# One fused scan-and-attention kernel: wider VectorE operations, B transposed in SBUF, A's x in four transposes, PSUM banks by table, a new static order

## The chip, the cores and the metric

The kernel runs on one core of a Trainium2 chip. A core has five engines with a queue each: TensorE (PE; its weight loads are listed as PEld), VectorE (DVE), ScalarE (ACT), GpSimd (POOL) and SyncE (SP), which here issues almost all DMAs. They share the on-chip memory SBUF (128 partitions), and PE writes to PSUM, which has 8 banks of 512 f32 a partition. Each engine works through its own instructions in program order, and waits at an instruction until what it needs is there. The metric is the device time of one execution in microseconds (us), lower is better.

## The reference

Two independent blocks read their own x of 2048 x 448 in bf16; their outputs stand side by side in a 2048 x 896 result.

```python
# A: a diagonal complex state space, 448 states
B_bar = ((Lam_bar - 1.0) / Lam)[:, None] * Bmat        # Lam_bar = exp(exp(log_dt) * Lam)
Bu = jnp.einsum("bld,pd->blp", x + 0j, B_bar)
for t in range(L):                                     # L = 2048
    h = Lam_bar[None, :] * h + Bu[:, t, :]
y = 2.0 * jnp.einsum("blp,dp->bld", hseq, Cmat).real + x * Dskip
# B: dilated local attention, 16 heads of 28, 8 keys at distance 0, 2, .. 14
q, k, v = ...                                          # x @ wqkv
logits = jnp.einsum("bhsd,bhswd->bhsw", q, kg) * scale # kg: the 8 keys of each position
attn = softmax(where(mask, logits, -1e9))
o = jnp.einsum("bhsw,bhswd->bhsd", attn, vg)
out = o @ wo
```

The factor `(Lam_bar - 1) / Lam` belongs to a state, so it may stand on a row of B or on a column of C.

## The kernel before

Position s = 16 q + j: q is one of 128 rows, j one of 16 columns (T = 16). A group g is four columns, a batch b two groups; batch 1 (j 8 to 15) is done ahead of batch 0. Channels come in KT = 4 tiles, three of 128 and one of 64.

**Block B.** x is transposed by DMA column by column group (`load`, L361). PE projects Q and K (L478, L485, L511); ACT or DVE evicts them from PSUM (helpers `copy` and `evict`: L215 and L217 on ACT, L219 and L221 on DVE) into the tile qk. For each of the eight distances w, DVE multiplies Q by shifted K (`prod`, L651 to L657) into a ring of three buffers of 4096 elements; two distances make one unit. Where the shift leaves the first column, a unit falls into pieces, as the positions wrap to the row above. PE sums over the channels with a 0/1 matrix (`summ`, L669, L675: logits). Softmax of a batch: a maximum (DVE, L698), subtraction (PE), exp (ACT, L708, with a table load ahead of it), a sum (PE, into sm_ps), reciprocal and product (DVE, L717 and L719), and a transpose of the result by DMA (L724). V is projected (L757) and evicted to vd; `halo` copies the rows that wrap. In `pv` DVE multiplies attn by vd (L814) and adds the products up (L817, L826, L829), and PE multiplies the sum by wo (L888, L895).

**Block A.** The states come in NM = 7 groups m of 64, real above imaginary part. `setup` computes the powers on POOL and ACT: exp and Sin on ACT (L1078, L1081), the products on POOL; Gd is the block matrix of the factor. `setup_weights` (L1149) multiplies B by Gd on PE, 28 matmuls into ps_b (L1161), and 7 evictions make Bcat. `powers` (L1170) builds for each m the block matrices of 15 powers of Lam_bar in one DVE operation of 1920 elements (pw, L1177). `scan` (L1186) runs in levels: B times x for the four residues i of j modulo 4 (L1227, L1236), then combining steps on PE with pw (L1246, L1253, L1263, ... L1281), each followed by an eviction on ACT (L1243, L1250, L1260, L1267, L1274); then back down (L1298, L1317, L1323), where a bank that was given up is filled again by a matmul with the identity (L1303, L1317). Of the scan's small buffers (e1, eA, eB, ubuf) there are NF = 3 sets. C is transposed by DMA (L1004) straight into Ccat, and `outputs` (L1405) multiplies h by C (L1424), adds x times Dskip by a diagonal matrix Dg (built on ACT, L1132; L1420), and for j from 12 on by DVE (L1401, L1436).

**What sets the order.** Every piece of work is a unit in a planner (`add`, L116). The order of all engines is a written-out list ORDER: an entry's value modulo 1000 is the unit, and the thousands choose the engine where a unit may run on either. A unit that comes earlier in the list stands earlier on its engine. PSUM is one double bank (tag W: logits, the scan's pairs) and six single banks (tag s) in rotation.

```python
for i in ORDER:
    u = self.units[i % 1000]
    u.on = u.eng[i // 1000]
```

SP's queue holds, in this order: x of B with A's two B loads among it, A's x in 15 transposes of four blocks and one of a rest (L974, L969, L977), the small loads, wo, vd's halo, attn's transpose, C, and later the outputs.

Of the kernel before, what the change touches and what calls it, by code (L numbers as in the profile page):

```python
# [32 lines left out]
QW = 2 + NCH  # L33
LV2 = ((1, 2, 3), (4, 8, 12), (16, 32, 48))
# [4 lines left out]
NF = 3  # L39
# [166 lines left out]
class Ctx:  # L206
# [84 lines left out]
    def warm(self):  # L291

        nc, P = self.nc, self.plan
        self.pr = self.pool.tile([NCH, 3 * 4096], bf16, name="prods")
        self.pr_ring = Ring(3)
        self.pr_ring.get()
# [21 lines left out]
class PartB:  # L318
# [94 lines left out]
    def prep(self, u_warm):  # L413
# [135 lines left out]
        for b in (1, 0):  # L549
# [29 lines left out]
            self.k3[:, JB:T, 1:2], self.k3[:, JB:T, NCH:NCH + 1]), [self.u_k3[2], self.u_k3[3], self.u_kh[0], self.u_kh[1]], 0)  # L579

    def qk(self, b, prio):
        nc, pool, V, P, cx = self.nc, self.pool, self.nc.vector, self.plan, self.cx
        box = {}
# [5 lines left out]
        first = True  # L589
        for g in (2 * b + 1, 2 * b):  # L590
            par = g - 2 * b
            j0 = 4 * g
            for tp in (3, 2, 1, 0):
                ub = {}
                deps = list(self.u_q[b, par])
                ws = (W - 1 - 2 * tp, W - 2 - 2 * tp)
                for w in ws:
                    for j in range(j0, j0 + 4):
                        src = j - DIL * w
                        if src >= 0:  # L600
                            deps += self.u_k[src // 4]
                        else:
                            deps += self.u_k[(src + T) // 4] + [self.u_pad[(src + T) // 8]]
                w3 = () if tp > 1 else (ws[0] - 4, ws[1] - 4)
# [956 lines left out]
```

## Time and profile before

| what | value |
|---|---|
| median of 3 runs | 139.11 us (138.9 to 139.13) |
| span of the profiled execution | 136.8 us |
| granted TensorE clock | 1.00 |
| DMA, mean | 121 GB/s, 54.8% of 16 engines' span in its main queue |
| HBM read and written | 4.32 MB and 3.67 MB |

The profile is of one execution; its span is from the first to the last instruction and is 2.3 us less than the median of the runs. Of an engine the page gives busy time, its share of the span and the number of instructions; a row of 40 digits gives the busy share in tenths for each fortieth of the span (3.4 us). A group's row ends with busy time and the mean duration of one; where an engine overlaps its instructions, the step from one start to the next is shorter than that duration, and it is the step that counts in a sum.

### The profile page before, as it was taken

Reading aid. Unit: us, or ns where it says so; the run is one execution under the profiler, and the core shown is the slowest. Engines: PE = TensorE matmul, PEld = TensorE weight load, DVE = VectorE, ACT = ScalarE, POOL = GpSimd, SP = SyncE. Lnnn points to the kernel's source line nnn. Section 1 sums busy time; section 2 is a strip of 40 time slices with the busy share of each in tenths; the row PEclk is TensorE's granted clock in tenths of the full one; section 3 lists DMA queues with packets and bytes.
Section 4 is the critical chain, followed back from the end, with each engine's and each line's share of the span. In section 5 each row is a group of like instructions: output and inputs, shape, how many; then the busy total and the mean of one; then the engine's idle time right before and its main releaser. Section 6 shows DMA issues by size and latency. Waiting matters only on the chain.

```text
span 136.8 us, 2838 instructions
## 1 busy us (share of the span) xinstructions
PE 131.0 (96%) x1066; PEld 67.2 (49%) x1071; DVE 123.1 (90%) x134; ACT 88.3 (65%) x199; POOL 17.5 (13%) x69
## 2 busy tenths in 40 slices
PE   7999999999999999999999999999999999999890
PEld 2534335444455453656444564556665545545450
DVE  1379998999999999997999999999999999999950
ACT  3455588998554976757795998779546461433561
POOL 7489830025000000000000000000000000000000
PEclk9999999999999999999999999999999999999999
DMA  4968943647555524667999029460074425744263
GB/s 130 271 128 204 187 87 59 156 117 112 84 113 53 99 50 108 172 119 113 195 218 203 0 41 233 133 143 3 0 61 109 138 65 146 160 136 134 74 194 101
DMA packets 41694, 16.58 MB, mean 121 GB/s; under 512 B 33685, under 2 KB 41044, under 8 KB 41681
## 3 DMA queue, kind: packets, MB, share of 16 engines
q1 hardware_dynamic: 41618, 16.40, 54.8%
q8 instruction: 8, 0.13, 0.4%
q14 instruction: 5, 0.04, 0.1%
q10 hardware_dynamic: 63, 0.01, 0.0%
HBM read 4.32 MB, written 3.67 MB: 58 GB/s over the span
## 4 chain that ended last, share of the span: by engine, by line
DVE 39%; PE 38%; SPq 10%; issue 5%; ACT 3%; DMA 2%; DVEq 0%; ACTq 0%
DVE rb L817 12%; DVE prods L814 11%; SPq L363 7%; PE v_ps L757 6%; PE scb L1227 5%; DVE rb L814 4%; PE scp L1227 4%; PE logits L669 3%; DVE pw L1177 2%; DMA rb<-in_B_x_dram 2%; PE qk_ps L478 2%; DVE prods L653 2%; PE wo_ps L895 2%; DVE rb L826 2%; ACT qk L215 1%
## 5 line engine op out<-in xcount | busy, mean ns | idle before, releaser
L814 DVE TENSOR_TENSOR prods<-attn,vd 128x3584 bf16<-128x3584 bf16 x12 | 24.0, 2016 | 0.0
L817 DVE TENSOR_TENSOR rb<-rb,prods 128x3584 bf16<-128x3584 bf16 x11 | 22.2, 2018 | 0.1
L653 DVE TENSOR_TENSOR prods<-qk 128x3072 bf16<-128x3072 bf16 (+1 forms) x15 | 19.1, 1324 | 0.0
L215 ACT CAST qk<-wo_ps 128x448 bf16<-128x448 f32 (+1 forms) x16 | 8.2, 527 | 10.0 <-PE wo_ps L888 7.8
L478 PE MATMUL qk_ps<-rb 128*128 128x512 bf16 x60 | 14.4, 379 | 0.3 <-DMA rb<-in_B_x_dram 0.3
L1424 PE MATMUL y_ps<-Ccat,qk 128*128 128x448 bf16 x60 | 14.6, 352 | 0.0
L215 ACT CAST vd<-v_ps 128x448 bf16<-128x448 f32 x16 | 7.9, 540 | 5.2 <-PE v_ps L757 4.9
L1227 PEld LDWEIGHTS <-Bcat 128*128 128x128 bf16 x84 | 7.5, 100 | 7.4 <-issue 1.1
L1274 ACT CAST ubuf<-scb 128x64 bf16<-128x64 f32 x35 | 7.3, 220 | 5.9 <-PE scb L1281 3.5
L1424 PE MATMUL y_ps<-Ccat,h 128*128 128x448 bf16 x45 | 11.0, 353 | 0.0
L1227 PE MATMUL scb<-xaT_sb,Bcat 128*128 128x512 bf16 x42 | 10.9, 380 | 0.0
L757 PE MATMUL v_ps<-rb 128*128 128x448 bf16 x48 | 10.1, 353 | 0.0
L217 ACT ACTIVATE qk<-qk_ps 64x512 bf16<-64x512 f32 (+1 forms) x15 | 8.9, 599 | 1.5 <-PE qk_ps L485 1.0
L478 PEld LDWEIGHTS <-rb 128*128 128x128 bf16 x60 | 5.6, 97 | 7.4 <-issue 0.7
L657 DVE TENSOR_TENSOR prods<-qk 128x768 bf16<-128x768 bf16 (+3 forms) x18 | 9.1, 565 | 0.1
L1424 PEld LDWEIGHTS <-qk 128*128 128x128 bf16 x60 | 5.9, 98 | 5.4
L814 DVE TENSOR_TENSOR rb<-attn,vd 128x3584 bf16<-128x3584 bf16 x4 | 8.1, 2020 | 0.1
L888 PE MATMUL wo_ps<-wo_p,rb 128*128 128x448 bf16 x36 | 8.1, 353 | 0.0
L1177 DVE TENSOR_TENSOR pw<-Dm,spair 128x1920 bf16<-128x1920 bf16 x7 | 8.0, 1150 | 0.0
L1227 PE MATMUL scp<-xaT_sb,Bcat 128*128 128x512 bf16 x30 | 7.8, 381 | 0.0
L215 ACT CAST qk<-qk_ps 128x512 bf16<-128x512 f32 (+2 forms) x11 | 6.3, 585 | 2.3 <-PE qk_ps L485 1.1
L215 ACT CAST qk<-y_ps 128x448 bf16<-128x448 f32 (+1 forms) x9 | 5.6, 662 | 3.1 <-PE y_ps L1424 3.1
(197 smaller groups left out, 258.9 us busy)
## 6 DMA issues: line engine op xcount, KB each, us to landing
out_dram<-qk SPq DMA_DIRECT2D x32, 112.0 KB, 1.7
vd<-vd SPq DMA_DIRECT2D x3, 392.0 KB, 4.4
rb<-in_B_wqkv_dram SPq DMA_DIRECT2D x3, 336.0 KB, 4.4
qk<-in_A_x_dram SPq DMA_DIRECT2D x1, 448.0 KB
ra<-in_A_B_re_dram SPq DMA_DIRECT2D x1, 392.0 KB, 4.2
ra<-in_A_B_im_dram SPq DMA_DIRECT2D x1, 392.0 KB
rb<-in_A_C_re_dram SPq DMA_DIRECT2D x4, 98.0 KB, 2.9
rb<-in_A_C_im_dram SPq DMA_DIRECT2D x4, 98.0 KB, 3.9
```

The costliest lines, as they stand in the source:

```text
L215: nc.scalar.copy(out, in_)
L217: nc.scalar.mul(out, in_, scale)
L363: nc.sync.dma_start(self.xT[:, j], bass.AP(x.tensor, x.offset + j * D - DT, [[T * D, NCH], [1, KT * NCH]]), transpose=True)
L478: nc.tensor.matmul(out(n), lhsT=w(n, full, k), rhs=self.xT[:, j:j + 4, k, :], start=(not rfirst and k == 1), stop=(rfirst and k == KT - 1) ...
L653: V.tensor_tensor(out.rearrange("p i j k q -> p i (j k) q"), qq.unsqueeze(1).to_broadcast([NCH, 2, 4 * nk, NCH]), bass.AP(kk.tensor, kk.of ...
L657: V.tensor_tensor(jk(out[:, i, a:e]), qq, kk, op=ALU.mult)
L757: nc.tensor.matmul(box["ps"][:].rearrange("p h d -> p (h d)"), lhsT=self.xT[:, j, k, :], rhs=self.wv[:, k, :], start=False, stop=(k == KT ...
L814: V.tensor_tensor(tmp[i].rearrange("p (j d h) -> p j d h", j=8, d=DH), aa, self.vd[:, o:o + 8], op=ALU.mult)
L817: V.tensor_tensor(acc, acc, tmp[i], op=ALU.add)
L1177: V.tensor_tensor(t[:], self.o["Dm"][:].rearrange("p (a b) -> p a b", b=2).unsqueeze(1).to_broadcast([NCH, 2 * NPW, 32, 2]), self.sp[:, m ...
L1227: mt(box[i], lhsT=self.Bcat[:, k, m, :], rhs=self.xk(slice(i, None, 4), k), start=(i % 2 == 0 and k == 0), stop=False, **kw)
L1424: nc.tensor.matmul(ps, lhsT=h, rhs=self.Ccat[:, m, :], start=(m == 0 and not skip), stop=(m == NM - 1), skip_group_check=True)
```

## The change

1. **Products.** A unit is now four distances (a half, hf) of three channel tiles, 6144 elements; the fourth tile goes apart in units of 2048. K gets a halo of two columns (kTh, k3h) with the wrapped rows, so that fewer shifts fall into pieces. The ring is two buffers of 6144 and one of 2048. `summ` feeds PE 512 columns an instruction.
2. **PV.** Products are made for one or two pairs of distances (3584 or 7168 elements) side by side and then folded in halves (7168, 3584, 1792).
3. **B, C, Dskip.** Raw B is transposed inside SBUF by two DMAs (21 and 28 blocks) into Bcat; the 28 matmuls and 7 evictions go. C is transposed as it is (Craw); 7 matmuls with Gd and 7 evictions make Ccat. A's x comes by four transposes of 14 blocks; odd columns are then shifted by 64 channels against even ones, hence two B layouts and seven Dg tiles for four.
4. **ACT or DVE, ACT or PE.** `powers` may build a matrix on ACT, by 30 operations of 64 columns; two of seven are. A reload of a bank may be a copy on ACT in place of the identity matmul.
5. **Buffers and order.** NF is 5. PSUM is one tile of 8 banks, and a table (BANKS) gives each use its bank. ORDER is new throughout, and C's transpose stands behind v's projection.

```diff
-NF = 3
+NF = 5
+BANKS = [
...
-SPLIT = ((1, 3), (1, 2), (0, 3))
-PAIR = (0, 0, 0, 1, 0, 1, 0)
+CUT = {(3, 0): (2, 3)}
+PAIR = (0, 0, 0, 0, 0, 0, 0)
...
-        self.pr = self.pool.tile([NCH, 3 * 4096], bf16, name="prods")
-        self.pr_ring = Ring(3)
+        self.pr = self.pool.tile([NCH, 2 * QKM + QKR], bf16, name="prods")
+        self.pr_ring = Ring(2)
...
+        self.u_halo = cx.double(768, self.kTh[:, 0:KH, :, 2:QW], self.kT[:, T - KH:T, :, 0:NCH], [self.u_pad[1], *self.u_k[3]], 0)
...
+                        out = ub["pr"][:, p0:p0 + np_].rearrange("p i j k q -> p i (j k) q")
+                        qq = jk(q[:, j0:j0 + 4]).unsqueeze(1).to_broadcast([NCH, np_, 4 * nk, NCH])
+                        kk = jk(kh[:, KH + o:KH + o + 4, :, c:c + NCH])
+                        V.tensor_tensor(out, qq, bass.AP(kk.tensor, kk.offset, [kk.ap[0], [DIL * nk * QW, np_], *kk.ap[1:]]), op=ALU.mult)
...
+            for u0, nu in ((5, 1), (4, 1), (0, 2)):
...
+            last = first = P.add("DVE", vec2(4 * n1), lambda f=fold: f(4 * n1), muls, prio - 0.1 * r, mode="r")
...
+        def load(g):
+            nc.sync.dma_start(self.xT[:, g], bass.AP(x.tensor, x.offset + 4 * g * D, [[T * D, NCH], [1, 4 * D]]), transpose=True)
...
+                ps = box["ps"] = self.psum.tile([NCH, D], f32, name="ps_c", tag="s")
+                gd = self.Gd[:].rearrange("p (m h) a b -> p m (h a b)", h=2)[:, m]
+                nc.tensor.matmul(ps[:], lhsT=gd, rhs=self.Craw[:, m, :], start=True, stop=True, skip_group_check=True)
...
+        def turn(n0, n, c0):
+            nc.sync.dma_start(self.Bcat[:, n0:n0 + n], self.bX[:, c0:c0 + n * NCH], transpose=True)
+        self.u_bm = [P.add("SP", c, lambda a=a: turn(*a), [self.u_b], prio, lat=2.5)
+                     for c, a in ((3.9, (0, 28, 0)), (3.0, (28, 21, D)))]
...
+            if eng == "ACT":
+                for k in range(NPW):
+                    for h in range(2):
+                        nc.scalar.activation(t[:, 2 * k + h].rearrange("p a b -> p (a b)"), self.o["Dm"][:], ACT.Copy,
+                                             scale=self.sp32[:, h, m * NPW + k:m * NPW + k + 1])
...
+            def reload(eng, out, in_):
+                if eng == "ACT":
+                    nc.scalar.copy(out, in_)
+                else:
+                    mt(out, lhsT=cx.ident[:], rhs=in_, start=True, stop=False, **kw)
...
-            dx = [self.u_bc[m], u_pw, u_pad]
+            dx = [*self.u_bm, u_pw, u_pad]
...
+            b = left.pop(0)
+            v = banks[:, b:b + (2 if tag == "W" else 1), :].rearrange("p b c -> p (b c)")
```

What the new order does at three places, as each engine's list reads.

ScalarE, from V's last evictions ahead of the first exp (ex_sb) on, before. vd is V, xaT_sb is A's x, h and e are the scan's buffers:

```order
L217 ACTIVATE qk<-qk_ps 128x4x128 x2
L215 CAST vd<-v_ps 128x448 x12
L215 COPY xaT_sb<-xaT_sb 64x4x128
L215 CAST vd<-v_ps 128x448 x2
L708 ACT_TABLE_LOAD
L708 ACTIVATE ex_sb<-logits 128x1024
L215 CAST vd<-v_ps 128x448 x2
L215 COPY xaT_sb<-xaT_sb 64x4x128
L1243 CAST h_134<-scp_808 128x512
```

The same place now; pw is a power matrix, banks is PSUM:

```order
L224 CAST vd_436<-banks_61 128x448 x5
L1165 ACTIVATE pw_485<-Dm_205,sh_227 128x64 x30
L224 CAST vd_436<-banks_61 128x448 x6
L226 ACTIVATE qk_111<-banks_61 128x4x128
L1165 ACTIVATE pw_601<-Dm_205,sh_227 128x64 x30
L1245 CAST h0_135<-banks_61 128x512 x2
L226 ACTIVATE qk_111<-banks_61 128x4x128 x2
L1252 CAST e1_681<-banks_61 128x512
L693 ACT_TABLE_LOAD
L693 ACTIVATE ex_sb_696<-banks_61 128x1024
```

Sixty ACTIVATEs of two power matrices have come in among V's evictions; the last evictions of Q (qk), the scan's first two (h0) and the first exp stand behind them.

VectorE, around the reciprocal of the first softmax, before (prods are the products of Q and K, rsum is the reciprocal):

```order
L653 TENSOR_TENSOR prods<-qk 128x3072 x2
L657 TENSOR_TENSOR prods<-qk 128x256 x2
L657 TENSOR_TENSOR prods<-qk 128x512
L1177 TENSOR_TENSOR pw<-Dm,spair 128x1920
L653 TENSOR_TENSOR prods<-qk 128x3072
L653 TENSOR_TENSOR prods<-qk 128x1024
L653 TENSOR_TENSOR prods<-qk 128x3072
L657 TENSOR_TENSOR prods<-qk 128x256 x2
L657 TENSOR_TENSOR prods<-qk 128x512
L653 TENSOR_TENSOR prods<-qk 128x3072
L717 RECIPROCAL rsum<-sm_ps 128x128
```

And now, from the first product of the second batch to the second maximum (mx):

```order
L652 TENSOR_TENSOR prods<-qk 128x6144
L683 TENSOR_REDUCE mx<-banks 128x128
L652 TENSOR_TENSOR prods<-qk 128x6144
L652 TENSOR_TENSOR prods<-qk 128x2048
L652 TENSOR_TENSOR prods<-qk 128x6144
L702 RECIPROCAL rsum<-banks 128x128
L704 TENSOR_TENSOR attn_t<-ex_sb,rsum 128x1024
L652 TENSOR_TENSOR prods<-qk 128x3072 x2
L652 TENSOR_TENSOR prods<-qk 128x1024 x2
L1168 TENSOR_TENSOR pw<-Dm,spair 128x1920
L683 TENSOR_REDUCE mx<-banks 128x128
```

The reciprocal stands behind three products of 6144 of the second batch, and the two smaller ones of 3072 come after it; a power matrix has moved from ahead of it to behind it.

SyncE, from the end of B's x on, before (the two loads of A's B, L954 and L955, stand ahead of this, among B's x):

```order
L363 DMA_TRANSPOSE rb<-in_B_x_dram 128x4x128
L974 DMA_TRANSPOSE xaT_sb<-in_A_x_dram 128x4x128
L340 DMA rb<-in_B_wqkv_dram 128x3x448
L342 DMA rb<-in_B_wqkv_dram 64x448 x2
L974 DMA_TRANSPOSE xaT_sb<-in_A_x_dram 128x4x128 x10
L969 DMA_TRANSPOSE xa_rest<-in_A_x_dram 128x1x128
L974 DMA_TRANSPOSE xaT_sb<-in_A_x_dram 128x4x128 x3
L977 DMA_TRANSPOSE xaT_sb<-in_A_x_dram 128x3x128
L978 DMA xaT_sb<-xa_rest 64x128
L974 DMA_TRANSPOSE xaT_sb<-in_A_x_dram 128x4x128
L943 DMA dsk_raw<-in_A_Dskip_dram 3x128
```

And now:

```order
L372 DMA_TRANSPOSE rb<-in_B_x_dram 128x4x128
L349 DMA rb<-in_B_wqkv_dram 128x3x448
L351 DMA rb<-in_B_wqkv_dram 64x448 x2
L936 DMA ra<-in_A_B_re_dram 64x7x448
L937 DMA ra<-in_A_B_re_dram 64x448
L936 DMA ra<-in_A_B_im_dram 64x7x448
L937 DMA ra<-in_A_B_im_dram 64x448
L948 DMA_TRANSPOSE xaT_sb<-in_A_x_dram 128x14x128 x4
L1151 DMA_TRANSPOSE Bcat<-ra 128x21x128
L1151 DMA_TRANSPOSE Bcat<-ra 128x28x128
L925 DMA dsk_raw<-in_A_Dskip_dram 3x128 x2
```

The loads of A's B have moved from among B's x to behind V's weights, A's x is 56 blocks in four transposes, and B's own two transposes of 49 blocks follow it.

More of the change, by code (lines that the diff above doesn't have):

```diff
@@ L588, in qk, with pieces @@
         begun = set()
-        first = True
+        done = {}
+        def pieces(j0, hf, cut):
+            res = []
+            for p in range(4):
+                w = 3 - p + 4 * hf
+                o = j0 - DIL * w
+                o, c = (o, 2) if o >= -KH else (o + T, 0)
+                if res and p not in cut and res[-1][3] == c and res[-1][2] + DIL * res[-1][1] == o:
+                    res[-1][1] += 1
+                else:
+                    res.append([p, 1, o, c])
+            return res
         for g in (2 * b + 1, 2 * b):
@@ L667, in summ @@
-                    for kt in range(3):
+                    at = lambda h, i: lg[32 * i:32 * i + 32, 4 - 4 * h:8 - 4 * h, :].rearrange("p (b a) q -> p a b q", b=2)
+                    new = not rest and hf not in begun
+                    begun.add(hf)
+                    for h, z, k in ((0, cx.Z[:, 3, zs], 0), (1, cx.Zh[:, zs], 0)) if rest else [(hf, cx.Z[:, k, zs], k) for k in range(3)]:
                         for i in range(4):
-                            nc.tensor.matmul(at(tp, i),
-                                             lhsT=cx.Z[:, kt, zs], rhs=pr[:, :, i, kt, :],
-                                             start=(new and kt == 0), stop=(kt == 2), skip_group_check=True)
@@ L672, in summ @@
-                    if tp < 2:
-                        for z, t2 in ((cx.Z[:, 3, zs], tp + 2), (cx.Zh[:, zs], tp)):
-                            for i in range(4):
-                                nc.tensor.matmul(at(t2, i),
-                                                 lhsT=z, rhs=ub["p3"][:, :, i, 0, :],
-                                                 start=False, stop=True, skip_group_check=True)
-                    cx.pr_ring.put(ub["r"])
-                if split:
-                    near = [*self.u_q[b, par], *(x for j in range(j0, j0 + 4) for x in self.u_k[(j - DIL * ws[1]) // 4])]
-                    u = P.add("DVE", vec2(1536), lambda f=prod: f(only=0), near, prio, acq="PR")
-                    prods.append(u)
-                    u = P.add("DVE", vec2(1536), lambda f=prod: f(only=1), [*deps, u], prio)
-                else:
-                    u = P.add("DVE", sum(vec2(x[0]) for x in ops()), prod, deps, prio + (g % 2 == 0) * 0.1, acq="PR")
@@ L686, in qk @@
-                prods.append(u)
-                u = P.add("PE", 0.33 if tp > 1 else 0.55, summ, [u] + sums[:1], -2, rel="PR", acq="W" if first else None, mode="c")
+                            nc.tensor.matmul(at(h, i), lhsT=z, rhs=pr[:, :, i, k, :].rearrange("p (a b) q -> p a b q", a=2),
+                                             start=(new and k == 0), stop=(rest or k == 2), skip_group_check=True)
+                    if not rest:
+                        cx.pr_ring.put(ub["r"])
+                prods += units
@@ L838, in pv, with mul @@
-            lasts[r] = [last, last]
-            if 2 * b + r == 0:
-                last = P.add("DVE", cost, lambda: step(part=1), [last], prio - 0.1 * r)
-                lasts[r][1] = last
-            self.pv_last = last
-            if not hasattr(self, "u_first"):
-                self.u_first = last
+            g = 2 * b + r
+            pb = cx.pr[:, 0:8 * n1]
+            def mul(u0, nu, r=r, g=g, pb=pb):
+                o, w0 = 4 * g + DIL * u0, 4 * (u0 // 4) + 2 * (u0 % 2)
+                v = self.vd[:, o:o + 8]
+                aa = self.attn[b][:, w0:w0 + 2 * nu, :, r, :].rearrange("q y i h -> q (y i) h").unsqueeze(2).to_broadcast(
+                    [NCH, 8 * nu, DH, H])
+                vv = bass.AP(v.tensor, v.offset, [v.ap[0], [DIL * D, nu], *v.ap[1:]])
+                V.tensor_tensor(pb[:, w0 * n1:(w0 + 2 * nu) * n1].rearrange("p (u j d h) -> p u j d h", u=nu, j=8, d=DH),
+                                aa.rearrange("q (u j) d h -> q u j d h", u=nu), vv, op=ALU.mult)
@@ new lines, in fold, with half, acc @@
+            def fold(n, out=None, pb=pb):
+                V.tensor_tensor(pb[:, 0:n] if out is None else out, pb[:, 0:n], pb[:, n:2 * n], op=ALU.add)
+            def half(part, pb=pb):
+                a, t = (pb[:, c:c + 2 * n1].rearrange("p (y j c) -> p y j c", y=2, j=4)[:, :, 2 * part:2 * part + 2] for c in (0, 2 * n1))
+                V.tensor_tensor(a, a, t, op=ALU.add)
+            def acc(g=g, fold=fold):
+                fold(n1, self.res(g))
+            muls = []
+            for u0, nu in ((5, 1), (4, 1), (0, 2)):
+                o = 4 * g + DIL * u0
+                dd = []
+                for p in range(o, o + 8 + DIL * (nu - 1)):
+                    dd += self.u_vh[p] if p < HALO else [self.u_v[p - HALO]]
+                dd += self.pv_dep[0 if nu < 2 else 1] if hasattr(self, "pv_dep") else [
+                    *self.u_prod[0], *self.u_prod[1], *self.u_lg[0], *self.u_lg[1], *self.u_vm, *self.u_proj]
+                muls.append(P.add("DVE", vec2(2 * n1 * nu), lambda f=mul, u0=u0, nu=nu: f(u0, nu), dd + [self.u_attn[b], *deps],
+                                  prio - 0.1 * r))
+                if not hasattr(self, "u_first"):
+                    self.u_first = muls[0]
@@ new lines, in pv @@
+            last = first = P.add("DVE", vec2(4 * n1), lambda f=fold: f(4 * n1), muls, prio - 0.1 * r, mode="r")
+            if g > 0:
+                last = P.add("DVE", vec2(2 * n1), lambda f=fold: f(2 * n1), [last], prio - 0.1 * r, mode="r")
+                last = P.add("DVE", vec2(n1), acc, [last], prio - 0.1 * r, mode="r")
+                lasts[r] = [last, last]
+            else:
+                last = P.add("DVE", vec2(n1), lambda f=half: f(0), [last], prio - 0.1 * r, mode="r")
+                lasts[r] = [last, P.add("DVE", vec2(n1), lambda f=half: f(1), [last], prio - 0.1 * r)]
@@ L957, in loads @@
-        self.u_b = P.add("SP", 1.3, bload, [self.u0], prio=0.15, lat=6.4)
+            for rows, src in ((slice(0, PL), self.A_Bre), (slice(PL, NCH), self.A_Bim)):
+                nc.sync.dma_start(bX[rows, 0:NM], src.rearrange("(m p) d -> p m d", p=PL))
+                nc.sync.dma_start(bX[rows, NM], src[0:PL])
+        self.u_b = P.add("SP", 2.4, bload, [self.u0], prio=0.15, lat=6.4)
     def load_x(self, deps):
         nc, pool, P = self.nc, self.pool, self.plan
-        self.xT = pool.tile([NCH, T, KT, NCH], bf16, name="xaT_sb", tag="xT")
@@ L980, in first @@
-        def first():
-            self.rest = tail()
-        u0 = P.add("SP", 1.35, first, deps, 0.5, lat=2.3)
-        for j in (0, 4, 8, 12, 2, 6, 10, 14, 1, 5, 9, 13, 3, 7, 11, 15):
-            self.u_x[j] = P.add("SP", 1.36 if j < T - 1 else 1.9, lambda j=j: load(j), deps if j < T - 1 else [u0], 0.6, lat=2.3)
-        self.u_xx = {i: self.cx.double(512, self.xT[PL:NCH, i:T:4, 3, :], self.xT[0:PL, i:T:4, 3, :],
-                                       [self.u_x[j] for j in range(i, T, 4)], 0.5) for i in (2, 3)}
@@ L988, in xk @@
-    def xk(self, j, k):
-        return self.xT[:, j, k, :]
+        def load(g):
+            nc.sync.dma_start(self.xT[:, g], bass.AP(x.tensor, x.offset + 4 * g * D, [[T * D, NCH], [1, 4 * D]]), transpose=True)
+        self.u_x = [P.add("SP", 1.6, lambda g=g: load(g), deps, 0.6, lat=3.0) for g in range(4)]
+    def xk(self, i, k):
+        o = 7 * (i // 2) + (k if k == 3 or i % 2 == 0 else 4 + k)
+        rows = slice(0, NCH) if k < 3 else slice(0, PL) if i % 2 == 0 else slice(PL, NCH)
+        return o, rows
@@ L1364, in scan @@
             if not hold[2]:
-                u = P.add("PE", pe(1, 512), back1, [u], PRI["bk"] + m * 0.1, acq="s")
+                u = P.add(("PE", "ACT"), (pe(1, 512), act(512)), back1, [u], PRI["bk"] + m * 0.1, acq="s", until=-1.0)
             u = P.add("PE", pe(2, 256), s5, [u, u3], pc)
```

446 lines of the change are left out of this document (204 added, 242 removed), and 67 rows, old and new, of tables (BANKS, ORDER).

## The prediction

> **What bounds the kernel now.** I read the page first: busy time, slices, chain.
>
> ```profile
> span 136.8 us, 2838 instructions
> PE 131.0 (96%) x1066; PEld 67.2 (49%) x1071; DVE 123.1 (90%) x134; ACT 88.3 (65%) x199; POOL 17.5 (13%) x69
> PE   7999999999999999999999999999999999999890
> DVE  1379998999999999997999999999999999999950
> ACT  3455588998554976757795998779546461433561
> DVE 39%; PE 38%; SPq 10%; issue 5%; ACT 3%; DMA 2%; DVEq 0%; ACTq 0%
> ```
>
> Two engines are full: VectorE (DVE) has hardly a gap after the seventh slice, TensorE (PE) hardly one after the first, and the chain divides itself between them. A saving on one alone is worth little; and any engine that feeds both, ScalarE (ACT) above all, can take it back. ACT has room on average, but not in every stage. The windows of 20 us (busy time and instructions of PE, PEld, DVE, ACT, POOL):
>
> ```profile
> 60.00:80.00 20.00, 19.70 (x177) 10.55 (x178) 19.13 (x14) 15.41 (x45) 0.00 (x0) 1.00 0.74 137
> 80.00:100.00 20.00, 19.95 (x154) 10.86 (x152) 19.79 (x15) 15.64 (x45) 0.00 (x0) 1.00 0.39 94
> ```
>
> The clock is 1.00 throughout. Then the chain (start, length, work), for the steps of long operations and for the tail:
>
> ```profile
> 70.61 0.65 PE scb L1227 x3
> ...
> 111.10 2.04 DVE rb L817
> ...
> 120.18 1.94 DVE rb L817
> ...
> 127.03 1.08 DVE rb L829
> 128.11 1.01 DVE qk L1401
> ...
> 130.00 1.05 PE pt_o L864 x16
> 131.05 2.28 PE wo_ps L895 x12
> 133.40 0.53 ACT qk L215
> ```
>
> A 512-column matmul takes 0.216 us of PE, a 448-column one 0.19. A 3584-element bf16 operation takes 1.94 of DVE, 2.04 when it reads what the one just before it wrote. From the second half of the last fold (127.03) to the end are 9.8 us that the change leaves as they are. The median of the runs shown is 139.1 against this execution's span of 136.8; I add 2.3 to every span.
>
> **The change, part by part.** The groups that shrink:
>
> ```profile
> L1177 DVE TENSOR_TENSOR pw<-Dm,spair 128x1920 bf16<-128x1920 bf16 x7 | 8.0, 1150 | 0.0
> ...
> L215 ACT CAST Bcat<-ps_b 128x512 bf16<-128x512 f32 x7 | 4.0, 608 | 0.0
> ...
> L1161 PE MATMUL ps_b<-Gd,ra 128*128 128x128 bf16 x28 | 2.2, 219 | 0.0
> ...
> L1317 PEld LDWEIGHTS <-ident 128*128 128x128 bf16 x10 | 0.9, 99 | 0.9 <-issue 0.4
> ...
> L1303 PEld LDWEIGHTS <-ident 128*128 128x128 bf16 x6 | 0.6, 100 | 0.1
> ```
>
> *PE.* Sixteen reloads on the identity become 6 (10 go to ACT): 10 x 0.216 = 2.1 us less. The 28 small B matmuls (2.2 busy, about 0.056 apart) become 7 of 448 for C: 7 x 0.19 = 1.3 against 1.6. The logits instructions halve at twice the width. Counted by width over the order, PE's work falls from 120.0 to 117.5 us: **-2.5**.
>
> *DVE.* The elements of the products do not change, only their grouping, and with 3584 in 1.94 and the 1920 of a power matrix (pw) in 1.07, an element costs 0.52 ns and an instruction 0.07 us: 27 fewer (88 rows in the order for 115) give -1.9. Two of the seven power matrices go to ACT: -2.1. Some four evictions of 0.6 us and the wm copy go to ACT as well, and a halo copy comes: about -2.4. In sum **-6.4**.
>
> So far the span would shrink by 2.5 to 6.4. Now what pays for it. The front is set by SP's queue (start, issue time) and by landings:
>
> ```profile
> 9.26 0.65 SPq L954 DMA_DIRECT2D ra<-in_A_B_re_dram  x1
> 9.96 0.63 SPq L955 DMA_DIRECT2D ra<-in_A_B_im_dram  x1
> ...
> 22.07 1.26 SPq L363 DMA_TRANSPOSE rb<-in_B_x_dram  x1
> ...
> 26.51 13.49 SPq L974 DMA_TRANSPOSE xaT_sb<-in_A_x_dram  x10
> ...
> 69.63 4.38 SPq L1004 DMA_TRANSPOSE Ccat<-rb  x1
> ...
> 80.21 1.51 SPq L852 DMA_TRANSPOSE rb<-rb  x1
> ```
>
> ```profile
> L363 SPq DMA_TRANSPOSE rb<-in_B_x_dram x11: 1253/1265/1302, 4.0 to 22.1; - x11
> ...
> DMA to landing us min/median/max: 2.9/3.7/3.8
> ```
>
> The two A_B loads leave the place ahead of x (-1.4), so its last transpose is issued at 20.7 and lands at 20.7 + 3.7 = 24.4. By the order PE then has 3.7 us of group 0 (14 matmuls of 512 and a logits batch) and 4.0 us of v (21 of 448) until the sixth v stands in PSUM: 32.1, evicted by 32.5.
>
> *B's and A's transposes.* After the wv load (1.8) and four A_B loads (2.6) SP is at 26.4. Then come 4 x 14 blocks of A_x and 21 + 28 of B, 105 in all, in place of 16 transposes that took SP 24 us. At the 28-block row, 4.38/28 = 0.156 us a block, they take 16.4; with the 2.4 that x needs from the end of its issue to landing, Bcat is there at **45.2**. The 14-block row gives 0.108 and 40.1; the 4-block row 0.32 and 62, but there a fixed part is in each issue, which is why I take the 28-block row. Every first scan matmul waits for both B transposes, and PE reaches them at about 43 (below): a wait of 2 us.
>
> *The power matrices on ACT.* No row shows a 128x64 ACTIVATE with a scale per partition. The nearest, four of 128x128 and the 64- and 128-column evictions:
>
> ```profile
> L1132 ACT ACTIVATE Dg<-ident,dsk x4: 410/416/432, 81.6 to 82.5; 128x128 bf16<-128x128 bf16 x4
> ```
>
> ```profile
> 46.75 1.28 ACT L708 ACT_TABLE_LOAD   x1
> 48.05 1.02 ACT L708 ACTIVATE ex_sb<-logits 128x1024 bf16<-128x1024 f32 x1
> 48.97 0.96 ACT L215 CAST vd<-v_ps 128x448 bf16<-128x448 f32 x2
> ...
> 51.89 1.07 ACT L1243 CAST h<-scp 128x512 bf16<-128x512 f32 x2 [1.32 <-PE scp L1236]
> ...
> 57.71 0.21 ACT L1274 CAST ubuf<-scb 128x64 bf16<-128x64 f32 x1 [0.47 <-PE scb L1281]
> 57.82 0.38 ACT L1260 CAST eA<-scb 128x256 bf16<-128x256 f32 x1
> ...
> 59.06 0.27 ACT L1267 CAST eB<-scb 128x128 bf16<-128x128 f32 x1
> ```
>
> The four Dg start 0.30 apart; 64 columns less are 0.06 less (0.27 against 0.21): 0.245 each, 30 of them 7.35 us a matrix. The bounds are 0.11 (from the 64-column eviction at 57.71 to the next, 3.3 a matrix) and 0.30 (9.0). I take 0.245, since Dg is the same operation with the same kind of operand. [...]
>
> The chain on ACT, in its order: six v evicted at 32.5; first matrix to 39.9; six v at 0.49 (48.97: 0.96 for two) to 42.8; PE's next Q matmuls wait for the fourth of these (41.8) and end at 42.7, their eviction at 43.1; **second matrix to 50.4**; the first two h0 evictions (0.5 each) at 50.9 and 51.4; two Q evictions to 52.3; e1, table load, exp to 55.2. With a landing of 2.9 in place of 3.7 and 0.43 for a v eviction all of this is 1.4 us earlier. So h0 is there at about 50.5, whether Bcat came at 43 or at 47, where before it was there at 51.89.
>
> *What that does to DVE.*
>
> ```profile
> 18.00 1.83 DVE L651 TENSOR_TENSOR prods<-qk 128x1536 bf16<-128x1536 bf16 x2
> ...
> 56.36 0.94 DVE L717 RECIPROCAL rsum<-sm_ps 128x128 f32<-128x128 f32 x1
> 57.41 1.23 DVE L719 TENSOR_TENSOR attn_t<-ex_sb,rsum 128x1024 bf16<-128x1024 bf16 x1
> 58.55 3.69 DVE L657 TENSOR_TENSOR prods<-qk 128x768 bf16<-128x768 bf16 x6
> ```
>
> Its dense products can start at about 18, as before (18.00), when group 2's Q is evicted; up to the last 6144 product ahead of RECIPROCAL it has 27.6 us of work and would be there at 45.6. But that product needs the two Q evictions, and a product buffer that PE frees only behind the h0 matmul: 51 to 52.3, plus 3.3 of its own. RECIPROCAL, which also needs exp, starts at 54 to 56 instead of 56.36. I take **55**. From there to the second half of the last fold: 11 operations of 3584 (21.3), 8 of 7168 at 3.81 (30.5), 3.5 of 1792 (3.5), 4 matrices (4.3), two reciprocals and two attn_t (1.05 and 1.14 each, 4.4), a reduction (1.15), four products (4.5), a copy: 69.8, and 0.7 for seven that read what was just written. Before it was 127.03 - 56.36 = 70.7. Half a microsecond for the next reduction, whose logits PE ends no earlier than 63 (bounds 0 and 2): 55 + 70.5 + 0.5 + 9.8 = **135.8**, so 138.1.
>
> *Edits at no price.* The three more Dg (0.9), seven C evictions (3.4) and ten reloads (4.8) on ACT come between 55 and 100, where the windows show 15.5 of 20 busy and deferred v evictions come on top: some 9 of 45 us more, hidden by ACT's idle, and gone from the cover if ACT fills. C's transpose and wo's loads move back in SP behind attn's transpose, which waits for DVE; vd's second halo, the skip row and x's rows queue there too; wo is needed after 85, SP is through by 75. Five scan sets and the bank table free waits or make them: below nothing by up to the 6.8 us that PE waits in that stretch (next part), above it by about as much as a mis-ordered eviction, 1 to 2. I take nothing.
>
> **The rivals.**
> *PE becomes the bound (slower).* At the h0 matmul PE has 78.0 us of its work left; before, at the same matmul (52.9, behind the eviction of 51.89), it had 73.6, and took until 133.3: 6.8 of waits. From 50.5 with the same waits it ends at 135.3, and with the 3.5 behind it the span is 138.8: **141.1**. For it: ACT, between PE's scan steps, gets fuller. Against: more sets and banks. It decides once the waits pass 4 us (50.5 + 78.0 + 4 + 3.5 = 136), and is slower than before from 5 us on.
> *The matrices cost ACT little.* At the bound of 0.11, h0 waits for Bcat at 45.2 alone and is there at 47.7; RECIPROCAL starts at 52.5: 133.3, **135.6**; with Bcat at 42 too, 49.6 and 132.7. For it: Dm is half as wide as Dg's input. Against: the step of Dg.
> *Bcat comes late.* Beyond 48 each us counts: at 50, **140.5**. For it: SP's 105 blocks run without a gap. Against: they replace as many.
> *The saving stays.* If neither ACT nor Bcat holds, DVE's 6.4 are kept: 132.7, the second price above.
>
> **How the numbers follow.** The forecast (DVE behind ACT, 138.1; its own range 137 to 139.6, from 54 to 56 at RECIPROCAL and 0 to 2 at the reduction) has 0.45: 0.30 faster, 0.09 the same, 0.06 slower. Cheap matrices or a kept saving have 0.24, all faster. PE as the bound has 0.25: 0.01, 0.02 and 0.22. Bcat late has 0.06, of which 0.05 is slower. A measurement of this kernel can tell about 0.2% from no change, so 138.8 to 139.4 counts as the same. Faster 0.55, same 0.12, slower 0.33. The range takes in the cheap matrices with Bcat at 44 and PE with all its old waits: 134.4 to 141.2.
>
> **What would show it.** Right: an ACT row of 60 ACTIVATEs at some 0.25 apart, a gap of 4 to 6 us on DVE ahead of its last 6144 product, ended by ACT, and RECIPROCAL at 54 to 56. Wrong: that gap absent and RECIPROCAL near 50 (cheap matrices); PE's first scan matmul waiting beyond 48 for a DMA; or DVE with gaps after 65 while PE has none (PE the bound).

## The result, and the profile after

The changed kernel takes 160.1 us where the kernel before takes 139.12: a ratio of 1.151 (95% interval 1.148 to 1.154). Of its four runs (159.85, 160.41, 162.29, 162.96) the last two were in a slower state of the chip and are not counted. The forecast was 138.1, and the end of its range, 141.2, is missed by 19 us. The profiled execution (160.41) has a span of 158.6. First the page of the changed kernel (busy time, then the slices, 3.97 us each):

```profile
span 158.6 us, 2562 instructions
PE 133.0 (84%) x912; PEld 63.7 (40%) x912; DVE 117.3 (74%) x100; ACT 108.4 (68%) x279; POOL 17.5 (11%) x70
PE   7999999900009958959999999999999999999891
DVE  1547779990000977809979999999999999999720
ACT  3448899500036999999598699999886982444561
PEclk9999999975555997899999999999999999999999
DMA  4955538999940003684339864147110712454463
```

DVE's busy time came down much as forecast, from 123.1 to 117.3; PE's rose from 131.0 to 133.0, at a mean clock of 0.935. But the slices have a hole that no engine had before: PE stands still from the ninth slice to the twelfth, ACT from the ninth to the eleventh, DVE from the tenth to the thirteenth. Up to the eleventh the DMA engines are full, and PE's clock is down to half (0.50 from 35 to 45). All three wait, so the cause is a wait that they share. The view of waits of the changed kernel (engine, line, what it waited for; total, times, longest):

```profile
POOL vd L761 <- DMA dsk_raw<-in_A_Dskip_dram: 26.7, 1, 26.7
...
DVE prods L652 <- PE banks L666: 17.5, 3, 15.8
ACT vd L224 <- DMA dsk_raw<-in_A_Dskip_dram: 16.1, 1, 16.1
PE banks L736 <- ACT qk L226: 15.8, 1, 15.8
```

Read as a chain: DVE waits for PE's logits, PE for an eviction on ACT, and ACT, like POOL, at a write of vd for a DMA. That vd should need Dskip makes no sense as data; the Dskip loads are only the last that SP had issued when the wait ended (at 45.38). The rows of SP and ACT (two views of the changed kernel; start, length, what) show what stands ahead of them:

```profile
27.10 9.72 SPq L948 DMA_TRANSPOSE xaT_sb<-in_A_x_dram  x4
36.92 7.25 SPq L1151 DMA_TRANSPOSE Bcat<-ra  x2
```

```profile
29.53 0.41 ACT L224 COPY qk<-qk 128x256 bf16<-128x256 bf16 x1
46.04 0.53 ACT L224 CAST vd<-banks 128x448 bf16<-128x448 f32 x1 [16.10 <-DMA dsk_raw<-in_A_Dskip_dram]
...
51.03 7.26 ACT L1165 ACTIVATE pw<-Dm,sh 128x64 bf16<-128x64 bf16 x30
```

B's two transposes are issued until 44.17, the second lands 5.2 us after its start at 40.6, so at 45.8, and they read **ra**. And vd lies in the memory of ra: one line that the change did not touch allots it there.

```python
t = pool.tile([NCH, TJ * D], bf16, name="vd", tag="RA")
```

So V's first eviction may not write until the last reader of ra is through. Before, that reader was PE (28 small matmuls on raw B, from 21.8 to 29.7), done ahead of V's first eviction at 33.96; now it is a DMA at the end of a queue of 105 blocks. V's evictions block ACT's queue in program order (16.1 us), PE's projections find no free bank (15.8), and DVE no logits (15.8). The experiments test this.

### The profile page after: what moved, and what is told of

Its sections match the earlier page's. It is cut to its first block, busy times and chain, and to the rows that moved or that the text cites. A ratio compares the mean times of both kernels' runs of the same rounds, so it can differ in the third digit from the quotient of the medians.

```text
span 158.6 us, 2562 instructions
## 1 busy us (share of the span) xinstructions
PE 133.0 (84%) x912; PEld 63.7 (40%) x912; DVE 117.3 (74%) x100; ACT 108.4 (68%) x279; POOL 17.5 (11%) x70
## 3 DMA queue, kind: packets, MB, share of 16 engines
q1 hardware_dynamic: 46600, 17.84, 52.3%
## 5 line engine op out<-in xcount | busy, mean ns | idle before, releaser
L652 DVE TENSOR_TENSOR prods<-qk 128x3072 bf16<-128x3072 bf16 (+4 forms) x17 | 31.8, 1912 | 23.6 <-PE banks L666 17.5
L224 ACT CAST qk<-banks 128x448 bf16<-128x448 f32 (+5 forms) x40 | 22.2, 587 | 15.4 <-PE banks L1435 5.2
L793 DVE TENSOR_TENSOR prods<-attn,vd 128x3584 bf16<-128x3584 bf16 (+1 forms) x12 | 31.4, 2643 | 0.1
L1230 PE MATMUL banks<-xaT_sb,Bcat 128*128 128x512 bf16 x84 | 22.9, 391 | 0.0
L797 DVE TENSOR_TENSOR prods<-prods 128x7168 bf16<-128x7168 bf16 (+1 forms) x7 | 21.6, 3090 | 0.2
L224 ACT CAST vd<-banks 128x448 bf16<-128x448 f32 x16 | 7.8, 538 | 17.6 <-DMA dsk_raw<-in_A_Dskip_dram 16.1
L736 PE MATMUL banks<-rb 64*128 64x448 bf16 x16 | 2.6, 378 | 15.8 <-ACT qk L226 15.8
L489 PE MATMUL banks<-rb 128*128 128x512 bf16 x60 | 15.5, 399 | 0.1
L1435 PE MATMUL banks<-Ccat,qk 128*128 128x448 bf16 x60 | 14.6, 352 | 0.0
L1165 ACT ACTIVATE pw<-Dm,sh 128x64 bf16<-128x64 bf16 x60 | 14.5, 340 | 0.0
L743 PE MATMUL banks<-rb 128*128 128x448 bf16 x48 | 11.2, 381 | 0.0
L1435 PE MATMUL banks<-Ccat,h 128*128 128x448 bf16 x45 | 11.0, 353 | 0.0
L1230 PEld LDWEIGHTS <-Bcat 128*128 128x128 bf16 x84 | 7.7, 105 | 7.6 <-issue 2.6
L666 PE MATMUL banks<-prods,Zsel 128*32 128x512 bf16 x112 | 7.7, 399 | 0.1
```

The costliest lines, as they stand in the source:

```text
L224: nc.scalar.copy(out, in_)
L489: nc.tensor.matmul(out(n), lhsT=w(n, full, k), rhs=self.xT[:, j:j + 4, k, :], start=(not rfirst and k == 1), stop=(rfirst and k == KT - 1) ...
L652: V.tensor_tensor(out, qq, bass.AP(kk.tensor, kk.offset, [kk.ap[0], [DIL * nk * QW, np_], *kk.ap[1:]]), op=ALU.mult)
L666: nc.tensor.matmul(at(h, i), lhsT=z, rhs=pr[:, :, i, k, :].rearrange("p (a b) q -> p a b q", a=2), start=(new and k == 0), stop=(rest or k ...
L743: nc.tensor.matmul(box["ps"][:].rearrange("p h d -> p (h d)"), lhsT=self.xT[:, j, k, :], rhs=self.wv[:, k, :], start=False, stop=(k == KT ...
L793: V.tensor_tensor(pb[:, w0 * n1:(w0 + 2 * nu) * n1].rearrange("p (u j d h) -> p u j d h", u=nu, j=8, d=DH), aa.rearrange("q (u j) d h -> q ...
```

## Experiments

The kernel before took 138.64 us on the chip of the first four runs, 139.04 on that of the next three, then 138.99, 138.75 and 138.83. All ratios are to it.

**1. Raw B out of vd's memory.** It is loaded into the memory that C's transposed matrix takes later; nothing else changes.

```diff
-        self.bX = cx.ra[:, 1856:1856 + (NM + 1) * D]
+        self.CB = cx.pool.tile([NCH, (NM + 1) * D], bf16, name="Ccat"); self.bX = self.CB[:]
...
-        self.Ccat = pool.tile([NCH, NM, D], bf16, name="Ccat")
+        self.Ccat = self.CB[:, 0:NM * D].rearrange("p (m d) -> p m d", m=NM)
```

> The changed kernel with raw B loaded into the memory of Ccat (made 448 elements longer) instead of into ra, whose memory V's tile vd takes over; nothing else differs, the order is the same. Theory S (vd cannot be written until B's two transposes, which read ra, have landed): the first V eviction comes at about 31 us instead of 46, the gap of 15 us on PE, ACT and DVE and the slow clock behind it are gone, the first h0 matmul is at 50 to 51, and the time is 138 to 141 us. Rival D (V's evictions wait for the DMA queue as such, the small Dskip loads that the profile names): the gap stays, 159 to 162 us. Within theory S, if DVE behind ACT sets the end, 138; if PE's waits set it, 141.

Measured: 143.68, ratio 1.036 (1.033 to 1.039), span 141.5. The hole is gone, and with it 16.4 us of the time and 17.1 of the profiled span, more than the 15.8 that PE stood still. V's first eviction is back at 29.81. What is left is 3.6% over the kernel before, and above what was expected. ACT, PE and DVE of this kernel (three views) are the stage that the prediction worked out:

```profile
29.81 0.53 ACT L224 CAST vd<-banks 128x448 bf16<-128x448 f32 x1
...
32.42 1.53 ACT L224 CAST vd<-banks 128x448 bf16<-128x448 f32 x3 [0.50 <-PE banks L743]
33.84 7.27 ACT L1165 ACTIVATE pw<-Dm,sh 128x64 bf16<-128x64 bf16 x30
...
44.41 7.24 ACT L1165 ACTIVATE pw<-Dm,sh 128x64 bf16<-128x64 bf16 x30
51.56 1.05 ACT L1245 CAST h<-banks 128x512 bf16<-128x512 f32 x2
52.50 1.08 ACT L226 ACTIVATE qk<-banks 128x512 bf16<-128x512 f32 x2
53.47 0.58 ACT L1252 CAST e<-banks 128x512 bf16<-128x512 f32 x1
```

```profile
42.86 1.02 PE L522 MATMUL banks<-rb 128*128 128x512 bf16 x4 [2.22 <-ACT vd L224]
...
43.77 2.33 PE L489 MATMUL banks<-rb 128*128 128x512 bf16 x6
46.92 2.74 PE L1230 MATMUL banks<-xaT_sb,Bcat 128*128 128x512 bf16 x6 [0.82 <-DMA Bcat<-Ccat]
...
51.43 1.46 PE L1230 MATMUL banks<-xaT_sb,Bcat 128*128 128x512 bf16 x6
52.73 0.59 PE L1248 MATMUL banks<-h,pw 128*128 128x512 bf16 x2
53.25 1.48 PE L666 MATMUL banks<-prods,Zsel 128*32 128x512 bf16 x24
```

```profile
54.19 3.36 DVE L652 TENSOR_TENSOR prods<-qk 128x6144 bf16<-128x6144 bf16 x1 [4.61 <-ACT e L1252]
57.47 0.95 DVE L702 RECIPROCAL rsum<-banks 128x128 f32<-128x128 f32 x1
...
128.51 2.10 DVE L801 TENSOR_TENSOR prods<-prods 128x1792 bf16<-128x1792 bf16 x2
```

Six matmuls of L1230 take 2.74 and, later, 1.46: the granted clock is 0.78 in the window from 42 to 46, 0.50 from 46 to 50 and 0.87 from 50 to 54. An estimate from these, with the clock either at 1.00 or at 0.50, puts the fall some 1.3 us after the wait of 2.22 had ended, and the rise at about 51.

**2. The same cause from the other side.** Raw B stays in ra, but its two transposes go ahead of A's x on SP (units 141 and 140 of ORDER).

```diff
-    121, 136, 1119, 488, ...
+    121, 141, 140, 136, 1119, 488, ...
...
-    ..., 466, 153, 141, 140, 461, 481,
+    ..., 466, 153, 461, 481,
```

> The changed kernel with one thing moved: on SP, B's two transposes stand ahead of A's four x transposes instead of behind them; raw B still lies in ra. Theory S: B's transposes land some 10 us earlier (36 instead of 46), the first V eviction follows at 36 to 37, and with 10 us less of the gap and less of the slow clock the time is 147 to 152 us. Rival D (the small Dskip loads at the end of that queue, or the DMA traffic as a whole, is what is waited for): they end where they did, and the time stays within 2 us of 161.

Measured: 154.70, ratio 1.113 (1.109 to 1.118). Above the expected 147 to 152, as SP issued the transposes only at 31.2, 4 us behind the loads of raw B (the last ends at 27.2), and V's first eviction came at 39.87 and not at 36 to 37. But the direction holds, and the waits now bear the right name (view of waits of this kernel):

```profile
POOL vd L761 <- DMA Bcat<-ra: 21.0, 1, 21.0
...
ACT vd L224 <- DMA Bcat<-ra: 10.3, 1, 10.3
```

With experiment 1 this settles the cause: the wait moves with the transposes, and goes when raw B lies elsewhere.

**3. Power matrices back on DVE, on top of 1.** Entries 1306 and 1228 of ORDER become 306 and 228.

> As the run with raw B apart, and the two power matrices that ACT builds (60 ACTIVATEs) are built by DVE, in two operations at the same places of the order. If ACT's 14.5 us ahead of h0 and exp hold the scan and the softmax: h0 is ready at 48 to 49 instead of 50.5 (then behind Bcat's landing at 46), and the time is 1 to 3 us under that of the run with raw B apart. If DVE's own work is the bound: 0 to 2 us above it.

Measured: 142.15, ratio 1.025 (1.022 to 1.029): 1.5 us better than 1. But the profiled executions (142.69 here, 143.19 there) differ by only 0.5, and DVE's gap only shrinks from 4.61 to 3.38, since B is no earlier (PE's and DVE's rows of this kernel):

```profile
47.16 2.74 PE L1230 MATMUL banks<-xaT_sb,Bcat 128*128 128x512 bf16 x6 [3.64 <-DMA Bcat<-Ccat]
...
52.32 0.59 PE L1248 MATMUL banks<-h,pw 128*128 128x512 bf16 x2
52.85 1.48 PE L666 MATMUL banks<-prods,Zsel 128*32 128x512 bf16 x24
```

```profile
53.79 3.36 DVE L652 TENSOR_TENSOR prods<-qk 128x6144 bf16<-128x6144 bf16 x1 [3.38 <-ACT e L1252]
57.06 0.95 DVE L702 RECIPROCAL rsum<-banks 128x128 f32<-128x128 f32 x1
```

PE waits 3.64 us for Bcat, runs at about half clock again (0.57 from 46 to 50), and RECIPROCAL comes only 0.4 us earlier. So with ACT free, B's landing holds DVE nearly as long. The profile puts the end of DVE's gap down to ACT's eviction of e, but here that ended at 53.33, 0.46 ahead of the product. In both runs the product starts 0.94 behind the first of the 24 matmuls of L666 (53.25 and 54.19, 52.85 and 53.79): the first twelve of them (0.83) read the buffer that it needs, and they stand on PE behind L1248.

**4. The reloads back on PE, on top of 1.** Eleven entries of ORDER lose their thousand; the expectation says ten, but the trace of the changed kernel has eleven copies (L1304) on ACT.

> As the run with raw B apart, and the ten PSUM reloads that ACT makes are made by PE again, by matmuls with the identity at the same places of the order. If ACT is full between 55 and 100 us and holds PE's scan steps: 1 to 3 us under the run with raw B apart. If PE's own work sets the end there: up to 2 us above it (10 x 0.216). If neither: within 0.5 us.

Measured: 145.24, ratio 1.049 (1.045 to 1.054): 1.6 us slower than 1, for 2.4 of PE work added (11 x 0.216). So these eleven are better placed on ACT.

**5. Softmax ahead of the scan, on top of 3.** Q's last two matmuls and evictions, one logits batch, the subtraction and exp go ahead of the scan's first matmuls, which wait for Bcat; one line of BANKS changes with it.

```diff
-    503, 190, 175, 191, 192, 126, 162, 504, 193, 194, 176, 196, 195, 128, 197, 127, 198, 161, 199, 164, 163, 177,
+    503, 175, 126, 128, 127, 161, 176, 190, 191, 192, 162, 504, 177, 193, 194, 196, 195, 197, 198, 199, 164, 163,
```

> As the run with raw B apart and both matrices on DVE (142.15 us, span 140.9), with the static order changed in the middle only: Q's last two matmuls with their evictions, one batch of logits (12 matmuls), the softmax's subtraction and its exp stand ahead of the scan's first matmuls (which wait for Bcat until 47.2) and of the h0 evictions, not behind them; the scan's first tile takes another PSUM bank for that. If what is left of the loss there is that DVE's last 6144 product stands behind work that waits for Bcat (3.4 us of DVE idle, ended by ACT): that idle falls to under 0.5 us, RECIPROCAL starts at 53.5 to 54.5 instead of 57.1, and the time is 138.5 to 140. If PE's own waits set the end: within 1 us of 142.

Measured: 140.16, ratio 1.008 (1.005 to 1.011): 2.0 us better than 3 (on another chip; 1.7% by the ratios). DVE's gap is gone and RECIPROCAL starts at 53.98.

**6. The tail's order, on top of 3; and 7, both orders.** In 6 the first transposes of the last columns get bank 0 and go ahead.

> As the run with raw B apart and both matrices on DVE (142.15), with the tail changed only: the first transposing matmuls of the last group get PSUM bank 0 instead of 5, two later tiles swap banks for it, and the eviction of these matmuls stands ahead of three evictions on ACT that wait for output DMAs. If the tail's 12.0 us (9.8 before) come from the bank table, which makes these matmuls wait for an eviction that waits for a DMA: they start at 129.1 instead of 131.0 and the time is 1.5 to 2 us lower. If the tail is PE's work alone: no change.

> Both changes of order together. If they are independent, the gains add: 136.5 to 138.5, under the kernel before (138.6). If the later end of the one is taken up by a wait of the other: no better than the better of the two.

Measured: 6 takes 142.31, ratio 1.025 (1.022 to 1.028), no gain over 3 that the runs can tell. In its profile the transposes (L845) start at 130.03 where 3 has them at 131.09, behind a gap of 0.77, and PE's last matmul ends 1.05 earlier, which lies between the two expectations. 7 takes 139.74 (10 runs), ratio 1.006 (1.004 to 1.008): the gains do not add, and it is no better than 5 beyond the noise. Its ratio is the lowest of the changed versions, and still above the kernel before.

**8. The six remaining reloads on ACT too, on top of 7.**

> e7_mid_tail with the six reloads that were left on PE (identity matmuls of 512 columns, 0.216 us each by their step) made ACT copies too; ten were there already. Theory A (once the waits of the front and the middle are gone, PE sets the end): PE's windows from 60 to 120 show 19.6 to 20.0 of 20 busy, so 6 x 0.216 = 1.3 us less work shortens the whole by 0.8 to 1.3, as ten reloads put back on PE cost 1.56; time 138.4 to 139.0, level with or under the kernel before. Rival B (DVE sets it): DVE's rows are the same, so no change, 139.5 to 140. Rival C (ACT takes it back: six copies of about 0.6 ahead of scan evictions that PE waits for): slower, 140 to 141, with PE waiting for ACT L1304.

Measured: 142.46, ratio 1.024 (1.022 to 1.026): 2.7 us slower than 7, so theory A's forecast fell and rival C came, and larger. The windows of 20 us, first of 7 and then of 8:

```profile
60.00:80.00 20.00, 20.00 (x164) 9.46 (x163) 18.32 (x12) 17.87 (x51) 0.00 (x0) 1.00 0.77 141
80.00:100.00 20.00, 19.55 (x163) 11.15 (x162) 19.86 (x11) 18.47 (x60) 0.00 (x0) 1.00 0.34 49
```

```profile
60.00:80.00 20.00, 18.91 (x153) 8.78 (x154) 18.98 (x12) 18.21 (x50) 0.00 (x0) 1.00 0.66 133
80.00:100.00 20.00, 17.82 (x140) 9.75 (x140) 18.81 (x11) 19.38 (x63) 0.00 (x0) 1.00 0.25 49
```

Columns: window, length, then busy time of PE, PEld, DVE and ACT. In 7 ACT has 1.5 to 2 of 20 us to spare. Six copies more (0.6 each) fill it to 19.4 in the second window, and PE stands idle 2.8 us more in the two, for 1.3 of work saved. In these 40 us PE's waits, all for ACT, come to 3.0 us, 1.6 of them for the copies (L1304); in 7 they were 0.3. DVE's last folds start 0.6 later, the end comes 1.9 later: behind the folds PE sets the end.

**9 and 10. A pair of V's projections into PE's last wait for Bcat, on top of 7.** The 1.66 us of PE work at 53 goes to 47; 10 also puts exp (177) ahead of the scan's first matmuls. The line of 10 is shown, against that of 7; the banks of later tiles change too.

```diff
-    503, 175, 126, 128, 127, 161, 176, 190, 191, 192, 162, 504, 177, 193, 194, 196, ...
+    503, 175, 126, 128, 127, 161, 176, 493, 494, 496, 177, 190, 191, 192, 162, 504, 497, 495, 193, 194, 196, ...
```

> e7_mid_tail with one pair of V's projections (8 matmuls of 448 columns, 1.66 us of PE, there at 52.9 to 54.7) and its two evictions put ahead of the scan's first matmuls, where PE waits 1.22 us for B's transposes (47.79); the later uses of banks 0 and 3, 1 and 2 are exchanged. Nothing is left out. Theory A (what is left over the kernel before is PE's idle time between 35 and 55, since PE is full from 60 to 120): the 1.2 us come off the end, 138.4 to 139.0. Rival B (the path from the RECIPROCAL on DVE sets the end, and it does not see this wait): no change, 139.5 to 140. Rival C (the two V evictions of 0.5 stand ahead of h0's on ACT, and V's 1.66 is longer than the wait, so the first h0 comes later by 0.4 to 1.4): 140 to 141.

> e9_v_fills with the exp of the first softmax ahead of the scan's first matmuls in ORDER. In e9 the exchange of banks gave the scan's second pair of sums (L1239) the two banks of the logits that exp had still to read: exp stood behind L1239 (a wait of 5.1 us), and took what was in those banks then, so e9 changes part of the first softmax and says nothing of the wait for B. Here exp reads first, and L1239 waits for it, if at all. Nothing is left out. Theory A (PE's idle time ahead of 55 is what is left): PE's 1.22 at the wait for B is filled, 138.4 to 139.0. Rival B (DVE's path does not see it): 139.5 to 140. Rival C (L1239, and with it h0, waits for exp, which ends at 49.0 where L1239 would start at 49.9 in e9's order; and two V evictions stand ahead of h0): 140 to 141.

Measured: 9 takes 143.16, ratio 1.031 (1.026 to 1.035), but computes part of the first softmax from other data, and exp waits for the scan (5.1 us), so it tells nothing of theory A. 10 takes 139.70, ratio 1.007 (1.005 to 1.009): the wait of 1.22 is filled (L1230 follows V's matmuls at once, at 47.70), and the time is that of 7. Rival B came: this wait alone was not what held. But PE gained less than 1.22: between 20 and 60 it idles 3.06 us, against 3.85 in 7.

## Why the prediction was wrong, step by step

**The step that failed** is the first of the front: "until the sixth v stands in PSUM: 32.1, evicted by 32.5". It asks when V's sums are there and not whether the tile they go to is free. The cost of turning B by DMA was counted by who needs Bcat (the scan's first matmuls, from 43 on), never by who needs the memory that it is read from. The rival "Bcat comes late" had the right transfer and the wrong waiter. In the changed kernel V's first eviction starts at 46.04; from there all that the prediction had from about 30 on follows 16 to 17 us late, and a part of it at half clock (0.50 from 45 to 50). Behind RECIPROCAL the length is the same: it starts at 74.55 with a span of 158.6, and at 57.47 with 141.5 in experiment 1, so 84.05 and 84.03 to the end.

**The other steps**, measured where that cause is taken away (experiment 1):

| step | forecast | experiment 1 |
|---|---|---|
| sixth V evicted | 32.5 | 33.95 |
| a power matrix on ACT | 7.35 | 7.27, 7.24 |
| Bcat there | 45.2 | 46.9 |
| gap on DVE ahead of its last 6144 product | 4 to 6 | 4.61 |
| RECIPROCAL | 55 | 57.47 |
| from it to the second half of the last fold | 71.0 | 72.1 |
| tail | 9.8 | 12.0 |
| span | 135.8 | 141.5 |
| from span to time | 2.3 | 1.7 |

- **The matrices' price** was right to 0.1 us. With the two back on DVE, experiment 3 took 1.5 us less.
- **B's price** was nearly right: the 105 blocks took 18.2 us of issue (26.75 to 44.98) where 16.4 were forecast, and 17.1 in the changed kernel, where the engines stood still.
- **RECIPROCAL, +2.5.** The gap was there, but ACT was not its only holder. In experiment 1 ACT and PE reach the h0 matmul together: h0's evictions follow the second matrix without a gap and end at 52.61, and PE, busy without a gap since Bcat came, is at L1248 at 52.73. Freeing ACT alone (3) gains 0.4 here; taking the product out from behind both (5) gains 3.1 more. So "whether Bcat came at 43 or at 47" is wrong: it did matter. Of the 2.5, 1.2 came from the front (sixth V at 33.95 for 32.5, then h0 at 52.6 for 51.4). The other 1.3 is the mis-sized term: the product was let go at 51 to 52.3, with the h0 matmuls, and had to wait for them (0.52) and for the twelve matmuls of L666 behind them, 1.46 from L1248 to its start. The prediction also left out the clock, which made L1230's first six 1.3 us longer (2.74 for 1.46).
- **The tail, +2.2.** The "9.8 us that the change leaves as they are" are not left as they are: the new order puts more of PE's work behind DVE's last product. Before, 16 transposes and 12 matmuls with wo stood there (the end of the prediction's chain). The chain of experiment 1 (start, length, work):

```profile
130.60 1.01 DVE qk L1411
131.61 0.60 PE banks L845 x8
132.21 1.32 PE banks L1435 x7
133.53 0.45 PE banks L845 x8
133.98 0.76 PE banks L876 x4
134.74 0.89 PE banks L845 x16
135.63 2.28 PE banks L876 x12
```

  From the end of that product (129.12 before, 131.61 here) to PE's last matmul were 4.2 us, and are 6.3; in experiment 6, where the first transposes stand ahead of the product's end, 5.4.
- **DVE's 6.4 us** were saved as busy time (5.8) and not as time; with the waits of the middle gone too, PE is nearly full from 60 to 120 (experiment 7: 20.00, 19.55 and 20.00 of 20), as the rival "PE becomes the bound" had it, and there ACT has no room for more of PE's work (8).
- **Two slips in the sums.** ACT got eleven copies, not ten. And "at 50, 140.5" should be 140.1 by the prediction's own steps: 2.5 behind Bcat, h0 comes at 52.5, 2.0 over 50.5.

**What stays open**: the last 0.6% of experiment 7. The windows of PE before and in 7 show where the profiled spans (136.8 and 138.8) part:

```profile
20.00:40.00 20.00, 19.94 (x205) 9.79 (x204) 19.12 (x27) 15.98 (x32) 2.82 (x4) 1.00 0.57 108
40.00:60.00 20.00, 19.70 (x218) 10.27 (x217) 19.86 (x23) 13.45 (x30) 0.00 (x0) 1.00 0.45 97
```

```profile
20.00:40.00 20.00, 19.09 (x137) 7.44 (x136) 19.15 (x16) 14.99 (x30) 2.52 (x5) 1.00 1.01 172
40.00:60.00 20.00, 17.06 (x122) 6.89 (x118) 19.03 (x11) 9.89 (x20) 0.00 (x0) 1.00 0.92 185
```

PE is busy 1.5 us less in 7 over the whole span (129.5 for 131.0) and idles 3.5 more, on balance all of it between 20 and 60: the difference is 2.0, that of the spans. That says where the time lies, not what would win it back: filling a part of it (10) gained nothing, and DVE keeps a wait for logits there (2.6 us ahead of 61.64). Which wait holds was not settled. No changed version beat the kernel before.

## What to carry to other kernels

When work moves from an engine to a DMA, ask of its source as well as of its result: whose memory is that, and who writes it next? Here two tiles that share memory by lifetime, ra and vd, turned a slow reader into a stall for a writer that has no data in common with it (16.1 us on ACT), and neither the diff nor an order of instructions shows that; list for every moved read the tile that comes after it in the same memory. And a tail is only "unchanged" if the order of the engine that ends it is the same.

## What the runs showed of the hardware

In two of the runs PE's clock fell to half behind a wait of little more than 2 us, 2.22 and 2.27. In experiment 1 the row of windows (length, PE, PEld, DVE, ACT, POOL, clock, DMA share, GB/s) reads:

```profile
42.00:46.00 4.00, 3.14 (x12) 1.05 (x11) 3.28 (x3) 3.75 (x12) 0.00 (x0) 0.78 1.17 223
46.00:50.00 4.00, 3.18 (x11) 0.88 (x12) 3.59 (x2) 4.00 (x18) 0.00 (x0) 0.50 0.58 159
```

The wait ahead of it was 2.22 us, from 40.64 on. In the changed kernel the clock fell in the same way behind a wait of 2.27 that ended at 60.04: 1.00 from 60 to 61, 0.60 from 61 to 62, 0.50 from 62 to 64. It did not fall behind one of 1.39, which ended at 69.37 (1.00 from 65 to 72). In experiment 7, with waits of 0.7, 0.7 and 1.2 between 40 and 60, it is 1.00 in that window. But in experiment 9 a wait of 2.44, which ended at 53.04, left it at 1.00 from 40 to 60, so the length of the wait does not decide alone. Just ahead of the waits of 2.22 and 2.27 stand matmuls of 128x32 (L666), ahead of that of 2.44 matmuls of 64x128 (L1239); whether that made the difference, no run here shows.

The stall of 15.8 us in the changed kernel cost more than its length. Behind it the clock was 0.50 until 50, 0.52 from 50 to 51 and 1.00 from 51 on. PE's work from its end to the last of L666 (47.23 to 57.78) took 10.55 us where experiment 1 (31.34 to 40.64) took 9.30.
